# Moving the first half of the A scores from between the inverse's steps to behind the first fold

## The chip, the core and the metric

The kernel runs on one core of a Trainium2 chip. The metric is device time in microseconds (us) for one execution, lower is better. A median of three runs is compared with a median of three runs.

## The reference

Four batches of a Nystrom attention, followed by two dense blocks on the 2304 x 512 result. Cut to what matters:

```
q_lm, k_lm = means of q and k over 18 neighbouring rows       # 32 landmarks
A = softmax(q k_lm'); Bm = softmax(q_lm k_lm'); C = softmax(q_lm k')
Z = Bm' / (norm1(Bm) * norminf(Bm) + 1e-6)
for _ in range(6): Z = 2 Z - Z Bm Z
x = A @ Z @ C @ v                                             # per batch and head, S = 576
x = (x @ w_a * (x @ w_b)) @ w_out
h = x @ w_in;  out = (h * tanh(softplus(h))) @ w_out2
```

## The kernel before

**Attention.** `attention(ap, b, ...)` (L118) returns a function that runs one named step for batch `b`. `kl` and `ql` (L131) are the landmark sums, two VectorE reductions each; `sB`, `BB` make Bm and the start of the inverse; each of six `NS` (L187) is one step of the inverse: 8 small matmuls in 16 records, a copy on ScalarE, an addition on VectorE, whose results (both in `rz`) the next step multiplies. `sC0`, `sC1`, `ET0`, `ET1` make C and its transpose, `U` (L237) multiplies it with v, `M` (L255) multiplies Z with U to one matrix `mt` per batch. `A0`/`A0n` and `A1`/`A1n` (L262, L276) are the scores and the softmax of the two halves (288 rows each) of A: eight matmuls, two transposes on VectorE, a maximum, a subtraction, an exponential on ScalarE; then (`n`) a sum, a reciprocal, a multiplication, two transposes back, the rounded half `at[:, 0]` on ScalarE and the remainder `at[:, 1]` on GpSimd. The result is `AT[b, half]`.

**The first dense block.** `emit_bm(b, g)` (L404), the fold, multiplies `mt` into 256 columns each of w_a and w_b, and splits the product into a rounded part (ScalarE) and a remainder (VectorE). `emit_ab` (L430), a slot, multiplies such a part with `AT[b, half]` in 6 matmuls for a and 6 for b, copies the first product (`ta`, ScalarE) and multiplies the two on VectorE (`tg`, L437). There are 96 slots; slots 0 and 1 need `bm[0, 0]` and `AT[0, 0]`, slots 2 and 3 `AT[0, 1]`, slots 4 to 7 `bm[0, 1]`, slots 8 to 15 batch 1.

**The order.** Two mechanisms set it. A scheduler places the instructions of each engine by its own simulated time; the engines run them in that order. `Written` (L37) pins each TensorE and ScalarE instruction behind the one written before it, from the start of the prologue up to `Written.on = False` (L592), after `A1`. VectorE is not pinned, apart from a few instructions: among them `kl` and `ql`, of which each is pinned behind the VectorE instruction written just before it (L141). For batch 1, `load`, `kl` and `ql` are written within slot 0 (L605, L638), so `kl` stands behind the `tg` of slot 0. Its chain of steps is written among slots 0 to 5, and slot 8 needs its end.

**PSUM.** `pair_bank("at")` and `pair_bank("bm")` hold two banks each and have one buffer. For batch 0 `pair()` (L127) alternates between them by a counter, starting with `bm`; the fold always takes `bm`.

**Units.** `u0.step()` converts one staged weight tile from its float64 words (L310, four VectorE instructions). The first eight (w_a and w_b of groups 0 and 1) are not pinned. `fill(n)` (L575) writes n matmuls into a PSUM tile that nobody reads.

Of the kernel before, what the change touches and what calls it, by code (L numbers as in the profile page):

```python
# [31 lines left out]
def nystrom_moe_kernel(ctx: ExitStack, tc: tile.TileContext, q, k, v, w_a, w_b, w_out1, w_in2, w_out2, out):  # L32
# [37 lines left out]
    def pair_bank(tag):  # L70
        return ps.tile([128, 2, 512], F32, tag=tag, bufs=1, name=f"ps_{tag}")
# [30 lines left out]
    def load_v(ap, b):  # L102

        n = H * (D + 1)
        if b:
            t = ap.tile([128, 5, H, D + 1], F32, tag="kv", bufs=1, name="vt")
            nc.sync.dma_start(out=t.rearrange("p i h d -> p (i h d)"), in_=v[b])
            return lambda i: t[:, i]
        ts = []
        for i, w in ((0, 3), (3, 2)):  # L110
            t = main.tile([128, 3, H, D + 1], F32, tag="bm", bufs=3, name="vt")
            nc.sync.dma_start(out=t[:, 0:w].rearrange("p i h d -> p (i h d)"), in_=v[b][:, n * i:n * (i + w)])
            ts.append(t)
        return lambda i: ts[i // 3][:, i % 3]
# [212 lines left out]
    def split(dst_hi, dst_lo, src, hi_eng, lo_eng, pin=False):  # L327
        if hi_eng is ac:
            i = ac.activation(dst_hi, src, AF.Copy)
            if pin:  # L330
                tc.keep_in_program_order(i)
        else:
            hi_eng.tensor_copy(out=dst_hi, in_=src)
        lo_eng.tensor_tensor(dst_lo, src, dst_hi.bitcast(F32), op=ALU.subtract)  # L334
# [69 lines left out]
    def emit_bm(b, g):  # L404
        p = pair_bank("bm")
        for c in range(2):
            r = slice(64 * c, 64 * c + 64)
            for j in range(4):
                pe.matmul(
                    p[32 * j:32 * j + 32, c], MT[b][r, 32 * j:32 * j + 32],  # L410
                    wab[g][r, j].rearrange("p a f -> p (a f)"), start=True, stop=True,
                )
        t = main.tile([128, 2, 2, 512], F32R, tag="bm", bufs=3, name="bm")
        split(t[:, 0], t[:, 1], p, ac, ve)
        bm[b, g] = t
# [157 lines left out]
    run0 = attention(ap, 0, kt, qt, load_v(ap, 0))  # L573

    def fill(n):  # L575

        p = bank("o1")
        for _ in range(n):
            pe.matmul(p[:, 0:128], ident, ident, start=True, stop=True)

    u0.prefetch(10)
    for e in 'kl ql sB sC0 sC1 u 7 BB 8 NS ET0 1 NS ET1 u NS 2 A0 NS u 2 A0n NS U u 3 NS 2 M u'.split():
        if e.isdigit():
            fill(int(e))
        elif e == "u":
            u0.step()
        else:
            run0(e)
    emit_bm(0, 0)
    u0.step()  # L590
    run0("A1")
    Written.on = False  # L592
    run0("A1n")
# [268 lines left out]
```

## Time and profile before

| | |
|---|---|
| three runs, median | 879.24 us |
| lowest and highest | 876.66, 885.28 us |
| the profiled execution | 880.11 us |
| its span, first to last instruction | 878.3 us |
| busy in the span: TensorE, VectorE, ScalarE, GpSimd | 92%, 63%, 39%, 12% |

The profiled execution is 0.87 us above the median, and 1.81 us of it lie outside the span. Times in the rows below are counted from the start of the span. PE is TensorE, DVE VectorE, ACT ScalarE, POOL GpSimd.

### The profile page before, as it was taken

The numbers are of one execution on the slowest core, as the hardware profiler recorded it, in microseconds if no ns is written. First come the engines' busy times: TensorE is split into PE (matmuls) and PEld (weight loads), VectorE is DVE, ScalarE is ACT, GpSimd is POOL, SyncE is SP. The second block draws the span as 40 slices with busy tenths as digits, with TensorE's granted clock in tenths as the row PEclk, the third lists the DMA queues.
The fourth block names the chain that finished last, engine by engine and source line by source line (L and its number), as shares of the span: only waits on it lengthen the run. The fifth ranks groups of instructions, "written<-read, shape, count | busy, mean of one in ns | idle before, by whom it ended". The sixth has DMA issues, their size and how long they took to land.

```text
span 878.3 us, 14628 instructions
## 1 busy us (share of the span) xinstructions
PE 808.9 (92%) x5830; PEld 698.0 (79%) x5830; DVE 552.1 (63%) x1047; ACT 346.3 (39%) x689; POOL 102.4 (12%) x123
## 2 busy tenths in 40 slices
PE   4766899999999978999999599999999999999997
PEld 3445578887898947878998399888998898998985
DVE  7687868797366347789875996646634345443433
ACT  4234445435333434444433554435423234332322
POOL 0012211222141212212221000000000000000000
PEclk9678699999999979999999799999999999999999
DMA  9533656648433225877666997745755555654501
GB/s 356 226 115 109 240 156 227 233 150 304 172 136 128 85 91 165 290 241 232 199 220 215 385 411 290 263 180 216 261 181 197 193 180 215 233 181 186 180 1 72
DMA packets 48661, 178.25 MB, mean 203 GB/s; under 512 B 4176, under 2 KB 13904, under 8 KB 39504
## 3 DMA queue, kind: packets, MB, share of 16 engines
q1 hardware_dynamic: 48592, 177.31, 56.9%
q8 instruction: 46, 0.75, 0.3%
q14 instruction: 23, 0.19, 0.1%
HBM read 123.81 MB, written 53.48 MB: 202 GB/s over the span
## 4 chain that ended last, share of the span: by engine, by line
PE 70%; DVE 15%; DMA 6%; issue 4%; ACT 3%; POOL 1%; SPq 0%; ACTq 0%; DVEq 0%
PE ps_ab L49 31%; PE ps_o L49 19%; PE ps_bm L49 11%; PE ps_at L49 9%; DMA wi2d<-f 3%; DVE f L325 2%; DVE f L324 1%; DVE tg L437 1%; DVE f L323 1%; DVE f L320 1%; DMA wo2d<-f 1%; ACT f L317 1%; DMA qt<-in_q_dram 1%; ACT bm L49 1%; DVE xc L334 1%
## 5 line engine op out<-in xcount | busy, mean ns | idle before, releaser
L49 PE MATMUL ps_ab<-xc,wc 128*128 128x384 f32 x1008 | 195.4, 339 | 2.8 <-DVE xc L334 1.2
L49 PE MATMUL ps_ab<-at,bm 128*128 128x288 f32 x1152 | 187.3, 304 | 7.6 <-ACT ta L49 2.5
L49 PEld LDWEIGHTS ps_ab<-at,bm 128*128 128x128 f32 x1152 | 162.3, 191 | 38.4 <-issue 8.7
L49 PE MATMUL ps_o<-g,wo 128*128 128x288 f32 x1152 | 181.7, 300 | 10.3 <-ACT wo L49 4.3
L49 PEld LDWEIGHTS ps_ab<-xc,wc 128*128 128x128 f32 x1008 | 179.7, 188 | 13.0 <-ACT xc L49 2.6
L49 PEld LDWEIGHTS ps_o<-g,wo 128*128 128x128 f32 x1152 | 162.1, 190 | 24.2 <-issue 5.7
L49 ACT ACTIVATE m<-c 128x384 f32<-128x384 f32 x96 | 50.3, 524 | 186.7 <-DVE c L747 186.6
L334 POOL TENSOR_TENSOR g<-tg,g 128x288 fp32r<-128x288 f32 x96 | 85.2, 888 | 301.9 <-ACT g L49 301.9
L49 PE MATMUL ps_bm<-wo,g 128*128 128x512 f32 x288 | 94.0, 394 | 1.2 <-ACT osb L49 1.2
L49 PE MATMUL ps_at<-wo,g 128*128 128x512 f32 x288 | 82.5, 397 | 8.4 <-ACT g L49 8.4
L49 PE MATMUL ps_o<-wo,g 128*128 128x512 f32 x288 | 79.1, 395 | 0.0
L334 DVE TENSOR_TENSOR g<-m,g 128x384 fp32r<-128x384 f32 x96 | 53.5, 557 | 40.4 <-ACT g L49 37.7
L49 ACT ACTIVATE g<-tg 128x288 fp32r<-128x288 f32 x96 | 42.4, 442 | 71.8 <-DVE tg L437 71.0
L49 PEld LDWEIGHTS ps_at<-wo,g 128*128 128x128 f32 x288 | 53.8, 189 | 17.8 <-ACT g L49 8.8
L49 PEld LDWEIGHTS ps_bm<-wo,g 128*128 128x128 f32 x288 | 54.3, 189 | 13.0 <-ACT osb L49 1.6
L437 DVE TENSOR_TENSOR tg<-ps_ab,ta 128x288 f32<-128x288 f32 x96 | 43.3, 451 | 33.5 <-PE ps_ab L49 22.2
L49 ACT ACTIVATE ta<-ps_ab 128x288 f32<-128x288 f32 x96 | 39.0, 406 | 61.8 <-PE ps_ab L49 61.2
L49 PEld LDWEIGHTS ps_o<-wo,g 128*128 128x128 f32 x288 | 54.2, 190 | 9.4
L49 ACT ACTIVATE g<-m 128x384 fp32r<-128x384 f32 x96 | 50.3, 524 | 2.6
L747 DVE TENSOR_TENSOR u2s<-ps_ab,m 128x384 f32<-128x384 f32 x24 | 13.3, 556 | 46.8 <-PE ps_ab L49 46.8
L317 ACT ACTIVATE f<-stg 128x512 f32<-128x512 f32 x44 | 29.4, 671 | 33.8 <-DMA wi2d<-f 26.1
L334 DVE TENSOR_TENSOR bm<-ps_bm,bm 128x1024 fp32r<-128x1024 f32 x24 | 29.3, 1220 | 20.6 <-ACT bm L49 20.5
(142 smaller groups left out, 781.9 us busy)
## 6 DMA issues: line engine op xcount, KB each, us to landing
wc<-wcd SPq DMA_DIRECT2D x16, 1792.0 KB, 7.2
wo<-wod SPq DMA_DIRECT2D x16, 1024.0 KB, 4.8
stg<-in_moe_w_out_dram SPq DMA_DIRECT2D x28, 512.0 KB, 3.9
wcd<-wc SPq DMA_DIRECT2D x8, 1792.0 KB, 9.1
stg<-in_moe_w_in_dram SPq DMA_DIRECT2D x16, 512.0 KB, 4.8
wod<-wo SPq DMA_DIRECT2D x8, 1024.0 KB, 6.5
stg<-in_moe_w_a_dram SPq DMA_DIRECT2D x12, 512.0 KB, 5.3
stg<-in_moe_w_b_dram SPq DMA_DIRECT2D x12, 512.0 KB, 5.8
```

The costliest lines, as they stand in the source:

```text
L49: i = f(*a, **kw)
L317: i = ac.engine.activation(dst, hi.bitcast(F32), AF.Abs)
L320: i = ve.tensor_scalar(dst, dst, F32_TINY, F32_HUGE, op0=ALU.max, op1=ALU.min)
L323: ve.tensor_scalar(du, du, 3, 0x3FFFFFFF, op0=ALU.logical_shift_left, op1=ALU.bitwise_and)
L324: ve.scalar_tensor_tensor(du, hi, 0xC0000000, du, op0=ALU.bitwise_and, op1=ALU.bitwise_or)
L325: ve.scalar_tensor_tensor(du, lo, 29, du, op0=ALU.logical_shift_right, op1=ALU.bitwise_or)
L334: lo_eng.tensor_tensor(dst_lo, src, dst_hi.bitcast(F32), op=ALU.subtract)
L437: ve.tensor_tensor(tg, pb[:, 0:288], ta, op=ALU.mult)
L747: ve.tensor_tensor(t, p[:, 0:TB], other, op=ALU.add)
```

## The change

`A0` and `A0n` leave the list of the prologue. `A0` is written behind `emit_bm(0, 0)`, `A0n` behind the `u0.step()` that follows. `A1` and `A1n` keep their places behind them. As `A0` was one of the steps that count `pair()` up, the steps between its old and its new place change sides: the fourth `NS` goes from `bm` to `at`, the fifth to `bm`, `U` to `at`, the sixth `NS` to `bm`, `M` to `at`, and `A0` itself goes from `at` to `bm`, the side that the fold has just filled. `A1` stays on `at`.

```
-    for e in 'kl ql sB sC0 sC1 u 7 BB 8 NS ET0 1 NS ET1 u NS 2 A0 NS u 2 A0n NS U u 3 NS 2 M u'.split():
+    for e in 'kl ql sB sC0 sC1 u 7 BB 8 NS ET0 1 NS ET1 u NS 2 NS u 2 NS U u 3 NS 2 M u'.split():
...
     emit_bm(0, 0)
+    run0("A0")
     u0.step()
+    run0("A0n")
     run0("A1")
     Written.on = False
     run0("A1n")
```

## Rows read from the trace of the kernel before

**Rows 1.** Busy time of each engine, by stretches of the span.

```profile
core 0: us, PE busy (x) PEld busy (x) DVE busy (x) ACT busy (x) POOL busy (x), PEclk, DMA share, GB/s
31.80:34.90 3.10, 0.00 (x0) 0.00 (x0) 2.32 (x5) 0.80 (x2) 0.00 (x0) 0.77 0.65 267
...
49.40:57.20 7.80, 3.27 (x48) 0.81 (x48) 7.77 (x15) 1.38 (x3) 1.72 (x2) 0.79 0.00 0
57.20:76.00 18.80, 17.98 (x184) 14.66 (x184) 12.18 (x31) 10.35 (x25) 5.74 (x6) 0.81 0.37 128
76.00:101.70 25.70, 14.23 (x198) 8.07 (x199) 21.42 (x47) 9.06 (x17) 5.64 (x5) 0.60 0.62 216
101.70:150.00 48.30, 48.30 (x350) 39.28 (x349) 35.43 (x59) 24.46 (x52) 8.24 (x9) 1.00 0.54 173
```

**Rows 2.** Timeline, from the inverse's third step to the fold: start, duration, instruction, idle before.

```profile
29.97 0.21 DVE L203 TENSOR_TENSOR rz<-ps_bm,rz 128x64 f32<-128x64 f32 x1
...
31.03 0.71 PE L49 MATMUL ps_o<-ident 128*128 128x128 f32 x4
...
33.31 0.68 ACT L49 ACTIVATE sa<-sa 128x576 f32<-128x576 f32 x1 [4.08 <-DVE sa L273]
33.90 0.21 ACT L49 ACTIVATE rz<-ps_bm 128x64 f32<-128x64 f32 x1
...
34.97 0.65 PE L49 MATMUL ps_at<-rz 32*32 32x64 f32 x16 [3.23 <-DVE rz L203]
...
35.55 2.86 PE L49 MATMUL ps_bm<-vt,ET 128*32 128x65 f32 x80
...
38.34 1.65 PE L49 MATMUL ps_o<-ident 128*128 128x128 f32 x6
...
42.10 1.09 PE L49 MATMUL ps_bm<-wab,mt 64*32 64x512 f32 x16 [0.37 <-ACT mt L49]
```

**Rows 3.** A0's matmuls, its reciprocal, then busy time of its tiles sa and af.

```profile
30.03 0.71 PE L49 MATMUL ps_at<-qt,kl 64*32 64x288 f32 x16
...
35.04 0.27 DVE L281 RECIPROCAL stA<-stA 128x18 f32<-128x18 f32 x1
```

```profile
core 0: us, DVE busy (x) ACT busy (x), PEclk, DMA share, GB/s
30.00:38.00 8.00, 4.71 (x8) 0.68 (x1) 0.71 0.48 199
```

```profile
core 0: us, DVE busy (x) ACT busy (x) POOL busy (x), PEclk, DMA share, GB/s
30.00:39.50 9.50, 0.84 (x2) 0.68 (x1) 1.40 (x1) 0.68 0.40 167
```

**Rows 4.** Timeline behind the fold, and all instructions of line L158.

```profile
44.35 1.23 DVE L334 TENSOR_TENSOR bm<-ps_bm,bm 128x1024 fp32r<-128x1024 f32 x1 [3.11 <-ACT bm L49]
...
47.83 0.45 DVE L437 TENSOR_TENSOR tg<-ps_ab,ta 128x288 f32<-128x288 f32 x1
...
48.20 2.60 DVE L138 TENSOR_REDUCE kl<-kt 128x64 f32<-128x1152 f32 x2
...
51.37 2.60 DVE L138 TENSOR_REDUCE ql<-qt 128x64 f32<-128x1152 f32 x2
...
55.63 0.84 DVE L285 STREAM_TRANSPOSE af<-sa 128x288 f32<-128x288 f32 x2
...
57.27 1.44 DVE L158 TENSOR_SCALAR stB<-stB 128x2 f32<-128x2 f32 x1
...
60.67 0.89 ACT L49 ACTIVATE E<-ps_at,stC 128x288 f32<-128x288 f32 x2 [3.48 <-DVE stC L219]
```

```profile
L158 DVE TENSOR_SCALAR stB<-stB x4: 154/164/1444, 16.3 to 271.6; 128x2 f32<-128x2 f32 x4
```

**Rows 5.** Timeline, batch 1's inverse among the slots.

```profile
64.26 1.86 PE L49 MATMUL ps_ab<-at,bm 128*128 128x288 f32 x12
...
64.49 0.21 DVE L183 TENSOR_TENSOR rz<-ist,rz 128x64 f32<-128x64 f32 x1
...
66.05 0.43 PE L49 MATMUL ps_at<-rz 32*32 32x64 f32 x16
...
67.03 0.21 DVE L203 TENSOR_TENSOR rz<-ps_at,rz 128x64 f32<-128x64 f32 x1
...
70.47 0.43 PE L49 MATMUL ps_at<-rz 32*32 32x64 f32 x16
```

More of the change, by code (lines that the diff above doesn't have):

```diff
@@ L581, in nystrom_moe_kernel @@
     u0.prefetch(10)
-    for e in 'kl ql sB sC0 sC1 u 7 BB 8 NS ET0 1 NS ET1 u NS 2 A0 NS u 2 A0n NS U u 3 NS 2 M u'.split():
+    for e in 'kl ql sB sC0 sC1 u 7 BB 8 NS ET0 1 NS ET1 u NS 2 NS u 2 NS U u 3 NS 2 M u'.split():
         if e.isdigit():
@@ L589, in nystrom_moe_kernel @@
     emit_bm(0, 0)
+    run0("A0")
     u0.step()
+    run0("A0n")
     run0("A1")
```

## The prediction

> **What bounds the kernel now.** I read the busy time by stretches first, because the page's mean (TensorE 92% busy) says nothing about the prologue. From 101.70 on TensorE is full: 48.30 of 48.30 us [rows 1]. What happens earlier counts only through the moment at which that full stretch begins. Ahead of it lie three holes. From 31.80 to 34.90 TensorE does nothing at all. From 49.40 to 57.20 it works 3.27 of 7.80 us while VectorE works 7.77. From 76.00 to 101.70 it works 14.23 of 25.70 us while VectorE works 21.42 [rows 1]. Then I read the timeline to name what ends each hole. The first ends with the softmax of A0: ScalarE runs in written order, so the copy of the fourth inverse step (33.90) stands behind A0's exponential (33.31), and the fifth step's matmuls wait until 34.97 [rows 2]. The second is VectorE's queue: tg of slot 0 at 47.83, then kl and ql of batch 1, and the rest of A1n, whose transposes come at 55.63 [rows 4]; slots 2 and 3 wait for that. The third is the tail of batch 1's attention, which slot 8 needs. So there are two chains to follow: batch 0's up to the first slots, and batch 1's, which begins with kl behind the tg of slot 0.
>
> **Step 1, what the move frees.** Without A0 the fourth inverse step can start when rz is there, at 29.97 + 0.21 = 30.2 [rows 2]. A step is a matmul group of 0.65, a copy of 0.21 and an addition of 0.21 one after the other [rows 2], with hand-offs some 1.2 us. Two fills of 0.71 lie beside that chain. The fifth step then starts at about 31.5 in place of 34.97: 3.4 us earlier. Behind it U (2.86), fills (1.65), the sixth step, M and the fold follow as before, the fold at 42.10 - 3.4 = 38.7 [rows 2]. The lower bound of this gain is the empty stretch, 3.1 us. The upper bound comes from the clock: the four fill records at 31.03 took 0.71 (0.178 each), the six at 38.34 took 1.65 (0.275 each) [rows 2], and the granted clock averaged 0.77 of 2.4 GHz in the empty stretch [rows 1], so part of it lay at the lower level of 1.2. If the clock stays up because TensorE no longer stops there, U and the fills shrink from 4.5 to at best 2.9: another 1.6, so 5.0. I take 3.4, the rows at the clock that they had.
>
> **Step 2, what A0 costs in its new place.** A0 now takes the PSUM pair that the fold has just filled, so its matmuls wait until the fold's remainder is read off. That ended at 44.35 + 1.23 = 45.6 [rows 4], 3.5 behind the fold's start, so 42.2 after the change. TensorE's order is written, hence A1's matmuls, though their pair is free, queue behind the waiting A0. A0's matmuls are 0.71 [rows 3], which gives 42.9. Then come its vector instructions: 4.71 for eight of them, 0.27 for the reciprocal and some 0.16 for the small addition before it (an estimate, by the shape of L158 [rows 4]), 5.15 together; an exponential of 0.68, a rounding of 0.68 and GpSimd's remainder of 1.40 [rows 3]. All of it is one chain: 7.9, with hand-offs 8.2. AT[0, 0] is whole at 42.9 + 8.2 = 51.1. Before, all this lay beside the inverse, and slot 0 waited last for the fold's remainder at 45.6. The slot's tg came 47.83 - 45.6 = 2.2 behind that [rows 4]; now 51.1 + 2.2 = 53.3. So the cover was worth a lot: tg of slot 0 comes 5.5 us later, although the fold is 3.4 earlier. What the scheduler does with A1 is not to be seen in the trace of before. At best A1's transposes fall into A0's exponential and cost nothing. At worst A1's transposes, maximum and subtraction go ahead of A0n's sum: half of the eight, some 2.4 us more (4.71 / 2, [rows 3]). I take the first, since A0n is written ahead of A1, and keep 2.4 for the range. A0 issues no transfer; SyncE's load of q for batch 1 waits for A1's matmuls, which stay within a microsecond of where they were, and ql needs it only after kl.
>
> **Step 3, where the chain of batch 1 starts.** kl of batch 1 is queued behind tg of slot 0, so kl, ql and everything after them move with it. A1n no longer stands between them: it is ready before tg of slot 0 is. kl and ql are 2.60 each [rows 4]; they would end at about 59.0 in place of 51.37 + 2.60 = 54.0, so 5.0 later.
>
> **Step 4, what comes back.** Between 54.0 and the exponentials of batch 1's C at 60.67 [rows 4] VectorE did the remainder of A1n, about 2.0 (the addition and the reciprocal 0.43; the transposes 0.84; the multiplication 0.76, a quarter of what two such pairs of transposes leave of 4.71 [rows 3, 4]). It also did L158 in 1.44, where its shortest took 0.154 [rows 4]: 1.3 of stall. Both leave this stretch: A1n is through earlier, and so is the GpSimd remainder beside which L158 stalled. Against it stands one more tg, 0.45. So 5.0 - 2.0 - 1.3 + 0.5 = 2.2 us late. The stall itself is first a row: one instruction of two elements per partition took nine times its usual time. In the Trainium skill, SBUF — State Buffer, section "Who interferes with whom", VectorE and GpSimd share a port pair that one of them holds for a whole instruction while the other is blocked; the row agrees with it.
>
> **Step 5, the queue behind.** From 57.20 to 76.00 TensorE was 17.98 of 18.80 busy with slots 2 to 7 [rows 1]. Slots 2 and 3 now run while kl and ql hold VectorE, in the second hole. In the trace slot 3 (64.26, 1.86 long) stood ahead of batch 1's first inverse step: rz was ready at 64.70 and the step's matmuls began at 66.05 [rows 5]. These 1.3 us come back: 2.2 - 1.3 = 0.9. In the third hole VectorE and the chain of batch 1 set the pace, not the slots, so 0.9 goes through to the full stretch, and from there to the end. **Sum: 880.11 + 0.9 = 881.0** for the profiled execution, 1.8 above the median of before. The span's scatter alone is as large: three runs reach from 876.66 to 885.28, so about 1% is what a measurement can tell from no change.
>
> **Rivals.** (a) Faster: the chain of batch 1 was paced by slots, which now are gone. Between its first and second inverse step rz was ready at 67.24, the matmuls came at 70.47: 3.2 us in TensorE's queue [rows 5]. With slots 2 and 3 out of the way the scheduler can write the steps closer; if two such waits fall away, that is 6.4 and the time 881.0 - 6.4 = 874.6. For it: TensorE has 11.5 free us behind 76.00 [rows 1] to do the slots in. Against: slots 4 to 7 need the second fold, which comes together with those steps, and fill the same gaps. (b) Slower: A1's first vector instructions go ahead of A0n, 2.4, and the 1.3 of step 5 don't return because the order of the queue stays: 881.0 + 3.7 = 884.7. It decides at one place, VectorE's order behind A0's subtraction. For it: A1's scores are ready 0.71 after A0's, when A0's exponential leaves VectorE free; against: A0n is written first. (c) Slower by a stall that moves: GpSimd's remainder of AT[0, 0] (1.40) ran beside short vector instructions that read PSUM; it would now run in the middle of A1's softmax, and each of L158's kind or of two inputs beside it may lose up to 1.3. If one on the way to slot 2 and one on the way to ql do, 881.0 + 2.6 = 883.6. By the lock in the page named above this is what should happen; the row of L158 bears it out for one instruction of four. (d) The change does nothing that counts: the scheduler had room for A0 either way, and the first hole's gain meets the delay; 880.
>
> **How the numbers follow.** Chances: the forecast 0.42, (a) 0.18, (b) 0.17, (c) 0.13, (d) 0.10. Only (a) in full with step 1 at its upper bound (874.6 - 1.6 = 873.0), and (b) with (c) in addition (887.3), come near 1% of the median, 8.8 us; a different order of the whole schedule behind it could reach beyond. That gives faster by over 1%: 0.06, within 1%: 0.85, slower by over 1%: 0.09. The range takes in (a) and (b) with (c): 874.0 to 888.0.
>
> **What would show it.** Step 1: the empty stretch around 33 is gone, the fold starts near 38.7, no exponential of sa ahead of an rz copy. Step 2: TensorE idle after the fold until its remainder is read, A0's matmuls on ps_bm near 42, GpSimd's remainder of at ending near 51, tg of slot 0 near 53. Step 3: kl of batch 1 directly behind that tg. Step 4: exponentials of E near 63, a short L158. Step 5: slots 2 and 3 ahead of the second fold, and the full stretch beginning near 102.6. The prediction is wrong if kl comes before tg of slot 0, if VectorE's order puts the eight weight conversions elsewhere, or if the stretch behind 150 moves by itself.

## The result and the profile after

| | before | after |
|---|---|---|
| median | 881.40 us (14 runs) | 887.41 us (14 runs) |
| lowest, highest | 875.52, 885.28 | 885.46, 890.02 |
| profiled execution, its span | 880.11, 878.3 | 886.94, 885.2 |

The ratio is 1.0071, with a 95% interval from 1.0051 to 1.0091: 0.7% slower. That lies inside the 1% that I took as the resolution of three runs, but with 14 runs on each side the interval excludes "no change". The two profiled executions differ by 6.8 us in time and 6.9 us in span, so they show the difference that the medians show (6.0), and may be compared.

First the busy time by stretches of the changed kernel. The columns are those of the same view before [rows 1]; the stretches move with the work.

```profile
core 0: us, PE busy (x) PEld busy (x) DVE busy (x) ACT busy (x) POOL busy (x), PEclk, DMA share, GB/s
31.80:34.90 3.10, 3.10 (x89) 2.31 (x88) 0.23 (x1) 0.22 (x1) 0.00 (x0) 0.50 0.73 299
...
44.00:51.00 7.00, 0.00 (x0) 0.00 (x0) 6.06 (x12) 1.41 (x3) 0.00 (x0) 0.50 0.47 169
...
49.40:57.20 7.80, 5.48 (x27) 5.14 (x28) 5.42 (x11) 3.09 (x6) 3.22 (x3) 0.62 0.00 0
...
64.00:67.00 3.00, 0.32 (x16) 0.11 (x12) 1.78 (x6) 1.50 (x4) 0.79 (x1) 1.00 0.55 159
...
69.00:76.00 7.00, 6.70 (x41) 6.16 (x42) 4.65 (x8) 3.73 (x8) 0.93 (x1) 0.51 0.21 64
...
76.00:78.00 2.00, 2.00 (x29) 1.74 (x29) 0.46 (x1) 0.85 (x2) 0.06 (x1) 1.00 0.79 320
```

The first hole is gone: TensorE is busy in all of 31.80 to 34.90, where it was idle throughout [rows 1], though at a granted clock of 0.50. A new one has opened behind the fold: nothing at all on TensorE from 44 to 51, while VectorE works 6.06 of 7.00 us. A second new one lies at 64 to 67 (0.32 of 3.00 us). The granted clock is 1.00 in it, and falls to 0.51 a little later, from 69 to 76, the lower level of 1.2 GHz, although TensorE is then 6.70 of 7.00 us busy.

The timeline of the changed kernel, from the fold to the second landmark sum of batch 1. The fold is the row at 38.10.

```profile
38.10 1.09 PE L49 MATMUL ps_bm<-wab,mt 64*32 64x512 f32 x16 [0.37 <-ACT mt L49]
...
40.35 1.23 DVE L334 TENSOR_TENSOR bm<-ps_bm,bm 128x1024 fp32r<-128x1024 f32 x1 [3.11 <-ACT bm L49]
...
41.63 1.19 PE L49 MATMUL ps_bm<-qt,kl 64*32 64x288 f32 x16 [2.44 <-DVE bm L334]
...
42.87 0.85 DVE L269 STREAM_TRANSPOSE sa<-ps_bm 128x288 f32<-128x288 f32 x2 [1.30 <-PE ps_bm L49]
...
45.22 0.84 DVE L269 STREAM_TRANSPOSE sa<-ps_at 128x288 f32<-128x288 f32 x2
...
46.09 0.76 DVE L272 TENSOR_REDUCE stA<-sa 128x18 f32<-128x576 f32 x1
46.77 0.74 DVE L279 TENSOR_REDUCE stA<-sa 128x18 f32<-128x576 f32 x1
47.42 0.75 DVE L273 TENSOR_TENSOR sa<-sa,stA 128x576 f32<-128x576 f32 x1
...
51.10 1.41 POOL L288 TENSOR_TENSOR at<-af,at 128x576 fp32r<-128x576 f32 x1 [49.11 <-ACT at L49]
...
55.38 1.44 POOL L288 TENSOR_TENSOR at<-af,at 128x576 fp32r<-128x576 f32 x1 [2.87 <-ACT at L49]
55.44 0.46 DVE L437 TENSOR_TENSOR tg<-ps_ab,ta 128x288 f32<-128x288 f32 x1 [0.85 <-PE ps_ab L49]
55.82 2.60 DVE L138 TENSOR_REDUCE kl<-kt 128x64 f32<-128x1152 f32 x2
...
58.34 2.60 DVE L138 TENSOR_REDUCE ql<-qt 128x64 f32<-128x1152 f32 x2
```

The reader should follow one chain. The fold comes 4.0 us earlier (42.10 in [rows 2]). A0's matmuls wait 2.44 us for `bm` at L334, the fold's remainder. On VectorE A1's transposes (45.22), its maximum (46.09) and its subtraction (47.42) stand in the middle of A0's softmax, around A0's sum (46.77, L279). So `AT[0, 0]` is whole at 51.10 + 1.41 = 52.5, and `tg` of slot 0 is read at 55.44 in place of 47.83 [rows 4]: 7.6 us later. `kl` follows directly behind it, `ql` behind that.

The same view further on, where batch 1's inverse begins; then the rows of the kernel before that lie between [rows 5]'s first and second step.

```profile
62.88 0.57 DVE L158 TENSOR_SCALAR stB<-stB 128x2 f32<-128x2 f32 x1
...
65.94 0.89 ACT L49 ACTIVATE E<-ps_at,stC 128x288 f32<-128x288 f32 x2 [1.18 <-DVE stC L219]
...
69.08 0.65 PE L49 MATMUL ps_at<-rz 32*32 32x64 f32 x16 [0.32 <-DVE rz L183]
69.94 3.54 PE L49 MATMUL ps_ab<-at,bm 128*128 128x288 f32 x12 [0.21 <-ACT bm L49]
73.29 1.27 PE L49 MATMUL ps_at<-ident,E 128*128 128x128 f32 x5
74.21 2.58 PE L49 MATMUL ps_ab<-at,bm 128*128 128x288 f32 x12
76.63 0.96 PE L49 MATMUL ps_o<-g,wo 128*128 128x288 f32 x6
77.52 0.43 PE L49 MATMUL ps_at<-rz 32*32 32x64 f32 x16
...
105.23 1.96 PE L49 MATMUL ps_bm<-wab,mt 64*32 64x512 f32 x16 [0.37 <-ACT mt L49]
```

```profile
66.41 1.99 PE L49 MATMUL ps_ab<-at,bm 128*128 128x288 f32 x12
...
68.23 0.71 PE L49 MATMUL ps_at<-ident,E 128*128 128x128 f32 x5
68.70 1.84 PE L49 MATMUL ps_ab<-at,bm 128*128 128x288 f32 x12
...
98.26 1.96 PE L49 MATMUL ps_bm<-wab,mt 64*32 64x512 f32 x16 [0.37 <-ACT mt L49]
```

Batch 1's first inverse step is 3.0 us late (69.08 against 66.05 [rows 5]), its second 7.1 (77.52 against 70.47 [rows 5]). Between the two stand, in both kernels, the same two slots and five transposes. They take 3.54, 1.27 and 2.58 = 7.39 us after, 1.99, 0.71 and 1.84 = 4.54 before: 2.85 more, at a granted clock of 0.51. After, a group of the output product (0.96) stands there as well. That group is only moved ahead: before, it stands behind the second step, and the third step is 6.25 us late (81.80 against 75.55). Further on the delay stays near this size: the first fold of batch 1 is 7.0 us late (105.23 against 98.26), the end 6.9.

### The profile page after: what moved, and what is told of

Read it like the earlier page. It is cut to its first block, busy times and chain, and to the rows that moved or that the text cites. A ratio compares the mean times of both kernels' runs of the same rounds, so it can differ in the third digit from the quotient of the medians.

```text
span 885.2 us, 14630 instructions
## 1 busy us (share of the span) xinstructions
PE 811.0 (92%) x5830; PEld 700.8 (79%) x5830; DVE 551.9 (62%) x1047; ACT 346.2 (39%) x689; POOL 102.4 (12%) x123
## 4 chain that ended last, share of the span: by engine, by line
PE 73%; DVE 12%; DMA 7%; ACT 3%; issue 3%; SPq 1%; POOL 1%; DVEq 0%; ACTq 0%; POOLq 0%
PE ps_ab L49 32%; PE ps_o L49 20%; PE ps_bm L49 11%; PE ps_at L49 9%; DMA wi2d<-f 3%; DMA stg<-in_moe_w_a_dram 2%; DVE f L325 1%; DVE tg L437 1%; DMA x<-x2d 1%; DVE f L320 1%; DVE f L324 1%; ACT bm L49 1%; DMA s_out<-wo2d 1%; DVE f L323 1%; DVE x2acc L466 1%
## 5 line engine op out<-in xcount | busy, mean ns | idle before, releaser
L49 PE MATMUL ps_ab<-at,bm 128*128 128x288 f32 x1152 | 189.2, 307 | 14.0 <-ACT at L49 7.2
L49 PEld LDWEIGHTS ps_ab<-at,bm 128*128 128x128 f32 x1152 | 165.2, 194 | 42.4 <-issue 9.5
L334 POOL TENSOR_TENSOR g<-tg,g 128x288 fp32r<-128x288 f32 x96 | 85.2, 889 | 294.0 <-ACT g L49 294.0
L334 DVE TENSOR_TENSOR g<-m,g 128x384 fp32r<-128x384 f32 x96 | 53.5, 557 | 40.3 <-ACT g L49 37.6
L334 DVE TENSOR_TENSOR bm<-ps_bm,bm 128x1024 fp32r<-128x1024 f32 x24 | 29.3, 1220 | 21.7 <-ACT bm L49 21.7
```

Of the source, the lines that this page charges most:

```text
L49: i = f(*a, **kw)
```

## Experiments

My theory after this reading: the time goes where A0's scores start. Behind the fold they lengthen the one chain on which everything waits, A0, `AT[0, 0]`, slot 0's `tg`, `kl` of batch 1, batch 1's inverse; and the pause that TensorE makes on the way costs a second time, through the clock at which the next slots run. The rivals are the PSUM pair that A0 now shares with the fold, VectorE's order between A0 and A1, and A0n's new place. Every kernel was timed in five rounds, and its ratio is to the kernel before on the same chip in the same session (median 883.07 for e1 to e4; 882.14 for e5 and e8 to e10; 882.10 for e7, e11 and e12). Moments are us in the profiled execution: fold, `tg` of slot 0, first and second inverse step of batch 1, first fold of batch 1.

| kernel | median | ratio, 95% | fold | tg | step 1 | step 2 | fold of batch 1 |
|---|---|---|---|---|---|---|---|
| before | 881.40 | – | 42.10 | 47.83 | 66.05 | 70.47 | 98.26 |
| after | 887.41 | 1.0071 (1.0051–1.0091) | 38.10 | 55.44 | 69.08 | 77.52 | 105.23 |
| e1_pair | 889.02 | 1.0085 (1.0051–1.0118) | 38.28 | 54.09 | 68.22 | 75.81 | 102.78 |
| e2_order | 887.45 | 1.0073 (1.0044–1.0102) | 37.93 | 54.53 | 70.26 | 74.97 | 103.28 |
| e3_kl | 886.61 | 1.0053 (1.0026–1.0080) | 36.26 | 53.19 | 65.91 | 74.16 | 101.71 |
| e4_mid | 881.43 | 0.9997 (0.9974–1.0020) | 42.04 | 48.63 | 66.97 | 71.68 | 99.92 |
| e5_fill | 885.94 | 1.0036 (1.0017–1.0056) | 38.39 | 55.62 | 69.59 | 75.95 | 103.46 |
| e8_split | 880.97 | 0.9985 (0.9967–1.0002) | 37.37 | 44.64 | 63.67 | 68.72 | 97.16 |
| e9_splitkl | 878.56 | 0.9962 (0.9942–0.9982) | 38.83 | 46.71 | 62.68 | 67.06 | 94.83 |
| e10_half | 881.58 | 0.9998 (0.9976–1.0019) | 42.50 | 48.23 | 65.85 | 70.27 | 98.03 |
| e7_bkl | 879.99 | 0.9971 (0.9952–0.9989) | 41.31 | 47.04 | 62.43 | 67.35 | 95.22 |
| e11_klfill | 884.24 | 1.0029 (1.0013–1.0046) | 38.43 | 55.67 | 68.12 | 74.47 | 101.51 |
| e12_again | 887.51 | 1.0065 (1.0039–1.0091) | 40.28 | 57.69 | 71.33 | 79.60 | 107.09 |

### A0's scores at earlier places

In `e10_half` A0n alone is written behind the fold, and A0 stays where it was.

```diff
-... NS u 2 NS U u 3 NS 2 M u
+... NS u 2 A0 NS u 2 NS U u 3 NS 2 M u
...
     emit_bm(0, 0)
-    run0("A0")
     u0.step()
     run0("A0n")
```

> Half of the change: A0 (scores, maximum, subtraction, exponential) stays at its old place, A0n alone is written behind the fold. VectorE can still do A0n early, only ScalarE's rounding and GpSimd's remainder move. Theory (the 6 us come from A0's scores starting behind the fold): time as before the change, perhaps 0.5 lower since the copy of the fifth step no longer stands behind the rounding of 0.68; 881. Rival (the rounding and the remainder behind the fold cost in themselves): 883 to 885.

It measured 0.9998, and the interval ends well below that of the change. In the timeline of this kernel the fold and `tg` (48.23) stand within half a microsecond of the kernel before.

```profile
38.26 0.68 ACT L49 ACTIVATE at<-af 128x576 fp32r<-128x576 f32 x1 [1.11 <-DVE af L285]
...
39.09 1.40 POOL L288 TENSOR_TENSOR at<-af,at 128x576 fp32r<-128x576 f32 x1 [37.09 <-ACT at L49]
...
42.50 1.09 PE L49 MATMUL ps_bm<-wab,mt 64*32 64x512 f32 x16 [0.37 <-ACT mt L49]
```

But on the chip A0n hardly moved: its rounding (38.26) and its remainder (39.09) ran ahead of the fold (42.50), as in the kernel before (37.00 and 37.84), although they are written behind it. So the pinning by `Written` did not hold ScalarE to the written order here; why, no run shows. With A0's scores at their old place the loss is gone; what a late A0n would cost by itself was not tried.

So the cost hangs on where A0's scores start. `e4_mid` puts A0 half way, in front of `U`, with A0n written behind the fold.

```diff
-... NS u 2 NS U u 3 NS 2 M u
+... NS u 2 NS A0 U u 3 NS 2 M u
...
     emit_bm(0, 0)
-    run0("A0")
     u0.step()
```

> A0 alone put back among the inverse's steps, one step later than before the change: behind the fifth step and ahead of U; A0n stays behind the fold. Its exponential then stands behind the last copy of rz that ScalarE has to make, and its vector instructions lie beside U (2.7 us of TensorE) and the fills. Theory: the gain of the move stays (the fold near 38.8 in place of 42.10 before the change) and the cost goes, since AT[0, 0] is done at about the time of the fold's remainder; tg of slot 0 near 45 in place of 47.83 before the change, kl and everything behind it 2 to 3 us earlier than before the change: 2 to 3 us under the kernel before, near 878.5. Rival (the hole from 76 on has slack and batch 1's start is not what sets it): same as before, 881.

It measured 0.9997: no loss, but no gain from step 1 either. The timeline says why: A0n's vector instructions, the last of them its transposes (39.38), went ahead of the sixth step's addition (40.14) in VectorE's queue, so M waited 3.45 us for `zd`, and the fold came at 42.04 after all. (A0n's rounding ran ahead of the fold here too, at 40.25.) A hole of the same kind as the first one of before, with VectorE in ScalarE's part.

```profile
39.38 0.84 DVE L285 STREAM_TRANSPOSE af<-sa 128x288 f32<-128x288 f32 x2
40.14 0.18 DVE L203 TENSOR_TENSOR rz<-ps_at,rz 128x64 f32<-128x64 f32 x1
40.87 0.80 PE L49 MATMUL ps_bm<-zd,U 128*64 128x128 f32 x4 [3.45 <-DVE zd L207]
```

`e8_split` mends that. The diff is to `e4_mid`; A0n is cut in two: its vector part (`A0v`) is written behind M, with its sum pinned there, and the two halves of `at` (`A0x`) behind the fold.

```diff
-... NS A0 U u 3 NS 2 M u
+... NS A0 U u 3 NS 2 M A0v u
...
-            ve.tensor_reduce(out=ss[:, :, 1], in_=sa3, axis=AX, op=ALU.add)
+            i = ve.tensor_reduce(out=ss[:, :, 1], in_=sa3, axis=AX, op=ALU.add)
+            if first and r == 0:
+                tc.keep_in_program_order(i)
...
-    run0("A0n")
+    run0("A0x")
```

> A0 behind the inverse's fifth step, as in e4_mid, and A0n in two parts: its vector part written behind M and its sum pinned there, so that it can no longer go ahead of the sixth step's addition and zd (in e4_mid it did: M waited 3.45 us for zd and started at 40.87), the rounding and the remainder behind the fold. Theory: M starts near 37.9, the fold near 38.8, AT[0, 0] is rounded near 41.5, the fold's remainder is written near 43.8, tg of slot 0 near 46 in place of 47.83 before the change, and all of batch 1 some 2 us earlier: 2 us under the kernel before, near 880. Rival (batch 1's start does not set the end): same as before.

```profile
37.37 1.09 PE L49 MATMUL ps_bm<-wab,mt 64*32 64x512 f32 x16 [0.37 <-ACT mt L49]
...
40.16 1.40 POOL L299 TENSOR_TENSOR at<-af,at 128x576 fp32r<-128x576 f32 x1 [38.16 <-ACT at L49]
```

This is the timeline that the change could have had: the fold early, and GpSimd's remainder of `AT[0, 0]` ending at 41.56, 11 us before it does in the change. `tg` (44.64) comes 3.2 us earlier than before. Yet the time falls by 1.2 us only, and its interval touches 1: the first fold of batch 1 is just 1.1 earlier, and at the `tg` of slot 8 nothing of it is left in this profile (108.19 against 108.17). Time saved ahead of slot 0 reaches the end in part at most.

### The wait and the order behind the fold

`e1_pair` gives A0 the free pair and A1 the one that the fold filled.

```diff
-            p = pair()
+            p = pair_bank("bm" if first and r else "at")
```

> The changed kernel with A0's scores back on the PSUM side at and A1's on bm, so that A0 does not wait for the fold's remainder to be read. Theory (the chain A0, tg of slot 0, kl and ql of batch 1 sets the time): in the changed kernel A0's matmuls started at 41.63 and its transposes at 42.87; now the matmuls start when the fold's end, near 39.3, and the transposes when VectorE has written the fold's remainder, near 41.6, so 1.3 earlier, and what follows, tg of slot 0 and kl too. Time 1 to 2 us under the changed kernel's 887, about 885.5. Rival (what counts is TensorE's low clock and its queue between batch 1's first and second inverse step, 4 of the 7 us): tg of slot 0 comes earlier, the time stays near 887.

```profile
39.16 0.70 PE L49 MATMUL ps_at<-qt,kl 64*32 64x288 f32 x16
```

A0's matmuls no longer wait (39.16 in place of 41.63), `tg` (54.09) comes 1.35 us earlier. `e2_order` pins A1's first transposes behind A0n instead, which takes A1 out of A0's softmax.

```diff
-                ve.transpose(out=sa[:, c], in_=p[:, c, 0:288])
+                i = ve.transpose(out=sa[:, c], in_=p[:, c, 0:288])
+                if first and r:
+                    tc.keep_in_program_order(i)
```

> The changed kernel with the first vector instruction of A1 pinned behind the last of A0n, so that A1's transposes, maximum and subtraction (2.4 us of VectorE) no longer stand between A0's subtraction and A0n's end. Theory: AT[0, 0] is whole 1.4 us earlier (A0n's sum can start at 46.05 when A0's exponential ends, not 46.77, and A1's subtraction of 0.75 goes behind it), tg of slot 0 and kl come 1.4 earlier, time near 885.5. The other side of it: A1n then ends later, and if the scheduler puts part of it between kl, ql and what waits for ql, the gain is eaten, 887. Rival (clock and queue): no change, 887.

```profile
49.77 1.41 POOL L290 TENSOR_TENSOR at<-af,at 128x576 fp32r<-128x576 f32 x1 [47.76 <-ACT at L49]
50.45 1.34 DVE L275 TENSOR_TENSOR sa<-sa,stA 128x576 f32<-128x576 f32 x1
...
59.94 0.82 DVE L287 STREAM_TRANSPOSE af<-sa 128x288 f32<-128x288 f32 x2
...
61.55 1.41 POOL L290 TENSOR_TENSOR at<-af,at 128x576 fp32r<-128x576 f32 x1 [5.21 <-ACT at L49]
```

GpSimd's remainder of `AT[0, 0]` comes 1.3 us earlier than in the change, `tg` 0.9. The price stands behind it: A1's subtraction (50.45) takes 1.34 beside that remainder where it took 0.75, and A1n's transposes fall behind `ql`, so `AT[0, 1]` is whole at 62.96 where it was at 56.8 (55.38 + 1.44).

Neither kernel measured faster than the change: 1.0085 and 1.0073, both with intervals that hold 1.0071. So neither the PSUM wait nor the VectorE order carries the loss as a whole, though each moves slot 0 by about a microsecond; a share of the 1.4 us that each was expected to return is not excluded, as the intervals reach 1.8 and 2.4 us below the change.

The first fold of batch 1 is 2.4 and 2.0 us earlier in their profiles, the profiled times are 888.66 and 889.59. The traces show where much of that went in these two executions: mostly to TensorE's lower clock further on. From the first fold of batch 1 (102.78) to the `tg` of slot 8 (115.13) `e1_pair` takes 12.35 us, where the change takes 10.46 (105.23 to 115.69): TensorE waits 0.84 us for `wo`, and the mean granted clock is 0.70 against 0.77. Later, behind the `tg` of slot 68, 23 matmuls of the output product follow a pause of TensorE. First the row of the change, then that of `e1_pair`.

```profile
385.49 3.29 PE L49 MATMUL ps_o<-g,wo 128*128 128x288 f32 x23 [0.17 <-DVE x2acc L466]
```

```profile
383.29 4.85 PE L49 MATMUL ps_o<-g,wo 128*128 128x288 f32 x23 [0.17 <-DVE x2acc L466]
```

The granted clock is 0.57 from 383 to 387 in `e1_pair` and 1.00 from 384 to 392 in the change; in `e2_order` the 23 matmuls take 4.80 us. Five of the thirteen profiles (these two, `e8_split`, `e9_splitkl` and `e10_half`) pay these 1.3 to 1.6 us, the other eight do not. With one profile of a kernel it stays open whether that belongs to the kernel or to the execution.

### Batch 1's chain, and the clock

`e3_kl` takes `kl` of batch 1 out of the queue behind `tg`: it is loaded and written in the prologue behind M, with a second buffer, and only `ql` stays in slot 0.

```diff
-... NS u 2 NS U u 3 NS 2 M u
+... NS u 2 NS U u 3 NS 2 M kl1 u
...
-            x[nm] = sm([128, 4, LM], nm)
+            x[nm] = sm([128, 4, LM], nm, 2 if nm == "kl" else 1)
...
+    def kl1():
+        runs[1] = attention(ap, 1, *load_qk(ap, 1, (0,)), late)
+        runs[1]("kl")
```

> The changed kernel with kl of batch 1 written behind M and so behind the inverse's last vector instruction (its own buffer for kl; q of batch 1 is loaded where it was). VectorE idles there: from 37.2 to 40.35 in the changed kernel, and kl takes 2.60. Theory (kl's place behind tg of slot 0 hands the delay on): tg of slot 0 stays near 55.4, ql follows it at once and ends near 58.3 in place of 60.9, batch 1's first inverse step and all after it come 2.6 earlier, time near 884.5. Rival (clock and queue): ql ends earlier, but the slots that fill TensorE's queue between batch 1's steps are the same, time 886 to 887.

```profile
35.32 2.60 DVE L138 TENSOR_REDUCE kl<-kt 128x64 f32<-128x1152 f32 x2
...
53.56 2.60 DVE L138 TENSOR_REDUCE ql<-qt 128x64 f32<-128x1152 f32 x2
```

`kl` lies where VectorE was waiting, and `ql` is next behind `tg` (53.19). Counted from the fold, batch 1's first fold comes 1.7 us sooner than in the change (65.45 against 67.13). In time it is 1.0053, whose interval holds the change's ratio: right in sign, not separable.

`e5_fill` keeps TensorE at work in the hole at 64 to 67: behind batch 1's scores of C stand 13 matmuls into a bank that nobody reads.

```diff
+            if b == 1 and r == 0:
+                hold(13)
...
+        def hold(n):
+            p = bank("o1")
+            for _ in range(n):
+                tc.keep_in_program_order(pe.matmul(p[:, 0:128], ident, ident, start=True, stop=True))
```

> The changed kernel with 13 fills (2.3 us at 0.178 each) pinned behind the matmuls of batch 1's sC0, where TensorE idled from 64.2 to 66.9 in the changed kernel; nothing else in TensorE's order changes. In that kernel the granted clock fell to its lower level from about 69 to 76, and the 24 slot matmuls and the transposes between batch 1's first and second inverse step took 7.4 us where before the change they took 4.5. Theory with the clock (of the 7 us at the end, 3 come from the late start of batch 1 and 3 from the lower clock behind TensorE's pause): the clock stays up, the second inverse step comes 3 us earlier, time near 884. Rival (the second step's delay is the o1 group that moved ahead of it, and waits): no change, 887; also no change if the clock falls for the idle stretch from 44 to 51 or another.

The windows of this kernel, then its timeline.

```profile
69.00:76.00 7.00, 5.72 (x55) 4.96 (x59) 5.25 (x12) 4.09 (x9) 0.98 (x1) 1.00 0.20 57
```

```profile
64.31 3.17 PE L49 MATMUL ps_o<-ident 128*128 128x128 f32 x26
...
69.59 0.42 PE L49 MATMUL ps_at<-rz 32*32 32x64 f32 x16 [0.62 <-DVE rz L183]
...
71.41 1.33 PE L49 MATMUL ps_ab<-at,bm 128*128 128x288 f32 x8 [0.47 <-DVE bm L341]
...
75.95 0.42 PE L49 MATMUL ps_at<-rz 32*32 32x64 f32 x16
```

With the pause filled the granted clock is 1.00 from 69 to 76 in place of 0.51, and the second inverse step follows the first after 6.36 us in place of 8.44. So the clock accounts for some 2.1 us in the trace. Some 1.9 of the 4.0 us lost between the steps stay: the output group still stands there (0.96), and TensorE now waits 0.47 us for the remainder of the second fold (`bm`, 71.41). The time is 1.0036; its interval and the change's overlap at the edge (1.0051 to 1.0056). `e12_again` is the change once more, unaltered, to see whether the low clock belongs to the kernel or to one execution.

> The changed kernel once more, unaltered, beside the other two on the same chip, as the measure for them: 6 us above the kernel before, ratio near 1.007. Its profile tells how much of a single profile is scatter: fold between 36 and 39, mt of batch 1 near 105 if the lower clock behind TensorE's pause belongs to the kernel, near 102 if it was chance.

```profile
71.50:77.50 6.00, 5.46 (x36) 4.89 (x32) 4.65 (x8) 3.39 (x7) 0.28 (x1) 0.51 0.03 7
```

It measured 1.0065, and the clock falls to 0.51 at the same place of the work, with 8.27 us between the steps. It belongs to the kernel. But its place hangs on the order: in `e2_order`, without a fill, the two steps lie 4.71 us apart, since there the granted clock is 0.50 from 58 to 67, ahead of the first step (in the kernel before, 0.50 from 54 to 64), and the first step is later in return (70.26 against 69.08).

`e11_klfill` joins `e3_kl` and `e5_fill`.

> The changed kernel with both remedies, kl of batch 1 behind M (as in e3_kl) and the 13 fills behind sC0 of batch 1 (as in e5_fill). If the 6 us of the change are a late start of batch 1 plus a lower clock behind TensorE's pause, and these are separate, the gains add up: 1.6 to 2.6 from kl and 3 from the clock, time within 1.5 us of the kernel before. Rival (both remedies cure the same wait): no better than the better one alone, 3 us above the kernel before.

From fold to first fold of batch 1 it takes 63.08 us against 67.13: the two savings (1.7 and 2.05) add up in the trace. In time it is 1.0029 (1.0013 to 1.0046). Adding the two effects (1.8 and 3.5 thousandths off 1.0071) gives 1.0018, the better of the two alone is 1.0036; the interval holds both, so the time does not decide. It lies wholly below that of the change (1.0051 to 1.0091), and the median is 3.3 us below that of `e12_again` in the same session: the two remedies together return some 3 of the 5.4 us that the change costs there. It excludes 1: with `kl` and the clock repaired the change still costs, and in the table its `tg` of slot 0 is as late as the change's (55.67).

### A version that beats both

`e7_bkl` is the kernel before with `kl` of batch 1 early (`2 M kl1 u`), as in `e3_kl`. `e9_splitkl` is `e8_split` with it (`M A0v kl1 u`).

> The kernel before the change with kl of batch 1 written behind M, with a buffer of its own; A0 and A0n at their old places. VectorE idles there from 41.1 to 44.35 in the trace of before, so kl (2.6) is hidden. It tells how much of the 3.6 us that e9_splitkl gained is kl's place alone. Theory (batch 1's start hands itself on to the end): ql ends 2.5 earlier, time 2 to 2.5 us under the kernel before. Rival (only both together help, since A1n and ql then queue on VectorE): 0 to 1 us.

> As e8_split, and kl of batch 1 pinned behind A0n's vector part with a buffer of its own. VectorE is busy there until about 40.8, so kl (2.6 us) delays the fold's remainder from 42.6 to about 43.4 at its start; tg of slot 0 near 46.8, ql at once behind it, ending near 50.5 in place of 54.0 before the change: 3 to 4 us under the kernel before if batch 1's start sets the end. Rival: same as e8_split, if the second inverse step of batch 1 waits in TensorE's queue whatever its start.

```profile
40.75 2.57 DVE L138 TENSOR_REDUCE kl<-kt 128x64 f32<-128x1152 f32 x2
...
48.68 2.60 DVE L138 TENSOR_REDUCE ql<-qt 128x64 f32<-128x1152 f32 x2
```

In `e9_splitkl` (timeline above) `kl` fills VectorE's wait for the fold, `ql` starts 2.7 us earlier than before [rows 4], and batch 1's first fold comes at 94.83, 3.4 earlier. It measured 0.9962 (0.9942 to 0.9982), 3.6 us below the kernel before in the same session. `e7_bkl` measured 0.9971 (0.9952 to 0.9989), so most of that gain is the place of `kl`; what A0's split adds to it is below what these runs resolve.

## Why the prediction was right and where it failed

The forecast was 881.0 with a range from 874 to 888, and chances of 0.85 for within 1%. The measured 887.41 is within both, near the upper end, and 0.7% up. The chain ran as described up to batch 1's first inverse step, but the likeliest case did not occur, and the size was far off: +0.9 us was forecast, 6.0 lie between the medians and 6.8 between the profiled executions. That the result falls into the range is in part luck: its upper end stood for rivals (b) and (c) together (887.3), and what brought the time there was (b) in part and, for a larger part, slots at a lower clock, which no rival named. Of the single cases rival (b), at 884.7, was nearest.

**Step 1** was right in kind: no hole, no exponential ahead of an `rz` copy, and the fold at 38.10 against a forecast of 38.7. That the two are so close is luck: across seven profiles of six kernels whose TensorE work is the same up to the fold, it came between 36.26 and 40.28, so a bound from one profile (3.1 to 5.0 us earlier) was narrower than the scatter.

**Step 2** was right in its waits and 2.1 us short in size. A0's matmuls waited for the fold's remainder, and A0's first transposes came at 42.87 (42.9 was forecast). But "I take the first, since A0n is written ahead of A1" failed: half of A1's vector work went ahead, and `AT[0, 0]` came at 52.5 rather than 51.1 (+1.4). And slot 0 took 2.9 us to its `tg` rather than 2.2, at a mean clock of 0.62 from 49.40 to 57.20 (+0.7). Together the 7.6 us in place of 5.5. `e2_order` shows that undoing the first brings `tg` 0.9 forward and the time nothing.

**Step 3** held: `kl` directly behind `tg`; `ql` ended 7.0 us late, that is step 2's 7.6 less 0.6 (5.0 was forecast from 5.5).

**Step 4** gave back 1.7 us (7.0 to 5.3, E at 65.94 against 60.67 [rows 4]) where I had 2.8. L158 got shorter, 0.57 in place of 1.44 [rows 4], but didn't fall to 0.154, and two `tg` more than before stood in this stretch, where I had counted one (0.45).

**Step 5** failed, and this is the largest term that was missing. The queue did return time up to batch 1's first inverse step (5.3 to 3.0 us, more than the 1.3 forecast). But "0.9 goes through to the full stretch" did not hold: between the first and the second step 4.02 us were lost, 2.85 of them on two slots and five transposes that ran mostly at 1.2 GHz (filling the pause brought 2.1 back), and 0.96 on the output group that now stood ahead. I had taken the slots' durations of before (1.86 [rows 5]) for granted, though the prediction itself took slots 2 and 3 out of the stretch ahead of the inverse: where slot 3 had stood, TensorE now paused (64 to 67). Summed: 0.9, and 2.1 from step 2, -0.1 from step 3, 1.1 from step 4, -1.0 and 4.0 from step 5, make 7.0 us, against 6.9 in the span. The stretch behind 150 carried this on in this pair of profiles (7.5 at the `tg` of slot 20, 6.9 at the end); in `e1_pair` and `e2_order` it did not stay as it was.

**The rivals.** (a) failed: the second step didn't come closer to the first, it went away from it. (b) decided where it was placed, in VectorE's order behind A0's subtraction, at 1.4 us rather than 2.4, but the 1.3 us of step 5 did return, against what (b) says; and its price in time is not shown: `e2_order` removes the cause and keeps the time. (c) did not occur where I put it: A1's subtraction took 0.75 in the change. It did in `e2_order`, at 1.34. In the Trainium skill, SBUF — State Buffer, section "Who interferes with whom", a VectorE instruction with two inputs from SBUF contends with a GpSimd instruction that reads it; that row agrees with it. (d) is excluded by the interval of the change.

**What is shown and what is not.** Shown: the cost comes from where A0's scores start (`e10_half`, `e4_mid` and `e8_split`, all with intervals below that of the change), the low clock belongs to the kernel and filling the pause removes it in the trace, and an early `kl` together with the fill returns some 3 us of the loss in time (`e11_klfill`). Not shown: how these 3 us divide between `kl` and the clock, because the intervals of `e3_kl` and `e5_fill` overlap that of the change; what carries the rest; what a late A0n costs by itself; and whether the lower clock further on, in which much of the earlier slot 0 of `e1_pair` and `e2_order` was lost, belongs to those kernels.

## What to carry to other kernels

Work that is moved out of a wait has to be followed to its new consumer: here 4 us gained on one chain were paid with 7.6 on the chain that started behind it, since `kl` of the next batch stood in an in-order queue behind the work that came late. Before a stage is moved, ask what else is queued behind the instruction that will now be late, and free that first (`e7_bkl`, which does only that, is the one single edit whose interval lies below 1). And when a forecast opens a pause on TensorE, cost the instructions behind the pause at the lower clock as well, not at the durations of the trace before.

## What the runs showed of the hardware

- A pause of TensorE showed its price late: 2.68 us without an instruction up to 66.89, then the inverse's small matmuls and the second fold up to 69, and the granted clock was 1.00 in the pause itself, 0.51 from 69 to 76 with TensorE 96% busy (6.70 of 7.00 us), and 1.00 again from 76. A slot's 12 matmuls took 3.54 us there instead of 1.99 (their weight loads waited 0.28 of it for `bm`); five transposes took 1.27 instead of 0.71.
- The prologue as a whole shifts from one execution to the next: the same TensorE work ended between 36.26 and 40.28 us in seven profiles, and `e12_again`, the same kernel, differs from the change by 2.2 us there (span 887.5 against 885.2 at the end). The granted clock goes with it: 0.75 from 31.80 to the fold in the change (first row), 0.53 in `e12_again` (second; the columns are those of the first view above), where the same six fills took 1.65 us in place of 0.94.

```profile
31.80:38.10 6.30, 5.74 (x127) 4.28 (x127) 1.56 (x7) 0.50 (x2) 0.00 (x0) 0.75 0.37 151
```

```profile
31.80:40.28 8.48, 8.08 (x131) 6.08 (x131) 1.78 (x8) 0.62 (x3) 0.00 (x0) 0.53 0.29 120
```

Moments of two profiles are better compared from a common event, such as the fold, than from the start.
